# Pooled attention and experts on one core: the last 64 queries of each head as one block of upper and lower halves

## The chip, the cores and the metric

The kernel runs on one core of one Trainium2 chip. TensorE (PE) multiplies matrices, with its weight loads shown as a row of their own (PEld); VectorE (DVE), ScalarE (ACT) and GpSimd (POOL) do the element work; SyncE (SP) issues most of the DMA transfers. The metric is the device time of the whole program in microseconds (us), a median over runs.

## The reference

```python
def _attn_ref(q, k, v):                                  # 8 batches, 8 heads, 1152 rows, head size 64
    q_pool = q.reshape(B, H, S // 2, 2, D).mean(axis=3)  # 576 pooled queries
    scores = scale * np.matmul(q_pool, k.transpose(0, 1, 3, 2))
    scores = scores - np.max(scores, axis=-1, keepdims=True)
    attn = np.exp(scores)
    attn = attn / (np.sum(attn, axis=-1, keepdims=True) + 1e-09)
    return np.matmul(attn, v)

# x: the attention's output as 4608 tokens of 512
logits = x @ w_gate + modality_bias[modality_id]
e_idx = np.argmax(logits, axis=1)                        # one of 8 experts
gate_w = softmax(logits)[rows, e_idx]
out[mask] = gate_w[mask, None] * (np.maximum(x[mask] @ w1[e], 0) @ w2[e])
```

## The kernel before, in words

**Pairs and steps.** The 64 heads are worked in 32 pairs p of two heads j. A pair takes 18 steps, one for each head and each chunk c of 128 keys (9 chunks). After the pairs come the experts, which the change does not touch.

**Scores.** `scores(p, j, r)` (L865 on) makes the exponentials of a block r of three chunks: 3 × 576 = 1728 columns, for 128 keys on the partitions. A pair has six such blocks; where they are counted below, r0 to r2 are those of head 0 and r3 to r5 those of head 1. The columns are cut into four score tiles t of BANK = 432 columns, each in one of three PSUM buffers. A tile is two to four matmuls, L903 and L904 (b1 and b2 are the two parts that give the scores more than fp16 precision). ACT takes the exponential of each tile (L905) into `Pe`, as 32-bit integers scaled by 2^25. The upper 16 bits of such an integer are read as one fp16 matrix, Ph. The lower 16 bits are multiplied by 2^-24 into a second fp16 matrix `Pl`: 1152 columns by ACT after tile t = 2 (L886), and 576 by DVE one step after tile t = 3 (L888). There are four buffers (Pe, Pl), `PT[i % 4]`.

**Value products.** `pv(p, j, c)` (L948) follows three steps later (LAG). For a chunk it takes the 576 queries in five groups g of 128 columns as the stationary operand and makes three products for each: L962 (Ph with the values' upper part `vh`), L963 (Ph with `vl`), L964 (Pl with `vs`). The fifth group holds only 64 queries of its own; the other 64 columns of that block are padding (zeros, set once at the start) or a neighbour's. All nine chunks add up in one PSUM tile `xp`, whose column 64 is the sum of the exponentials. `evac` (L971) then divides: DVE L980, a reciprocal, and L985 into `x2`. `split_x` (ACT L922) rounds the result, and for odd p a DMA transpose of it (L946) is issued on SP.

**Work for later pairs.** While pair p−2 is computed, pair p is prepared: `split_q` (POOL L655, pools the queries), `split_qh` (POOL cast L664 to `qh`, followed by two DMAs that copy `qh` into the block matrix `QB`, issued on SP), `split_lo` (POOL L692, three times), and for pair p+1's values POOL L783, twice. `maxpass(p)` (L824) multiplies QB with the keys (PE L836), DVE L837 takes the maximum over the keys; the row of maxima goes back by a small DMA (L817). These are placed by a table of step numbers: the cast at T_QH = −26, which is step 10 of pair p−2, the first matmul of maxpass at T_MAX = −24, two steps later.

**What sets the order.** PE, ACT, DVE and POOL run their instructions in the order in which the program writes them: ORD, three strings, gives each step's order of score tiles (s), value products (v), maximum matmuls (M) and due work (F), and the T_ tables say at which step preparation is due. SP's queue order is not written by hand; it is chosen when the program is scheduled. On all of these engines the queue is worked in order, so an instruction that waits holds up those behind it.

Of the kernel before, what the change touches and what calls it, by code (L numbers as in the profile page):

```python
# [22 lines left out]
P = 128  # L23
# [16 lines left out]
NR = 4  # L40
W3 = 3 * SQ
HELD = 3
BANK = W3 // 4
T_LIST = -127
PL = 2
RS = (4, 4, 2, 2)
# [117 lines left out]
class Router:  # L164
# [420 lines left out]
def attention(tc, ctx, att, ident, npairs, xpool, on_two, on_split, on_scale, jobs, side, set_pm, started, ahead, hip):  # L585
# [163 lines left out]
    def scales(p, pt):  # L749
        s = st[p]  # L750
        half = sm.tile([P, 1], I32, name="half", bufs=1)
        nc.vector.tensor_single_scalar(half, pt[:, 0:1].bitcast(I32), 24, op=ALU.logical_shift_right)
        sc = sm.tile([P, 2], I32, name="sc")
        power_of = lambda o, h, sign, e: nc.vector.tensor_scalar(o, h, sign * 2.0 ** 23, e * 2.0 ** 23, op0=ALU.mult, op1=ALU.add)
# [111 lines left out]
    def scores(p, j, r):  # L866


        s = st[p]
        b1, b2 = s["B1"], B2[p % 2]  # L870
        i = (p * 2 + j) * 3 + r
        assert free[i % NR] == 0, "the value products of these exponentials come too late"
        free[i % NR] = 3
        Pe, Pl = PT[i % NR]
        word = lambda dt, w: Pe.bitcast(dt).rearrange("p (n w) -> p n w", w=2)[:, :, w]
        s["P", j, r] = (word(F16, 1), Pl, i % NR)
        lows = LOWS_LAST if p == npairs - 1 else LOWS_LIST[P_LIST[p]] if p in P_LIST else LOWS if p else LOWS0
        lows = lows[i % len(lows)]
        up = lambda a, b: slice(D + a, D + b) if j else slice(D + W3 - b, D + W3 - a)
        for m in range(3):  # L880
            later_end((LAG if p else LAG0) + m, lambda m=m: pvq.append(pv(p, j, 3 * r + m)))

        def lower(eng, cols):
            low, rest = Pl[:, cols], word(U16, 0)[:, cols]
            if eng == 'A':
                nc.scalar.activation(low, rest, AF.Copy, scale=LOW)  # L886
            else:
                fast[0] = (nc.vector if eng == 'D' else nc.gpsimd).tensor_single_scalar(low, rest, LOW, op=ALU.mult)  # L888

        for t in range(4):  # L890
            need(p, *(("place",) if p else ()), "row5" if j == 0 and (p == 0 or p in TWO_ROWS) else "row9")
            pt = ps_sc.tile([P, 512], F32, name="psc")[:, 0:BANK]
            x0 = t * BANK if j else W3 - (t + 1) * BANK
            x1 = x0 + BANK
            ms = [(x0 // SQ, x0, min(x1, (x0 // SQ + 1) * SQ))]
            if ms[0][2] < x1:
                ms.append((ms[0][0] + 1, ms[0][2], x1))
            for n, y0, y1 in ms if j else ms[::-1]:
                c = 3 * r + (n if j else 2 - n)
                ks = slice(j * S + c * P, j * S + (c + 1) * P)  # L900
                q0 = 2 * S + j * SQ - n * SQ
                qs, o = slice(q0 + y0, q0 + y1), pt[:, y0 - x0:y1 - x0]
                nc.tensor.matmul(o, b1[:, ks], b1[:, qs], start=True, stop=False, skip_group_check=True)  # L903
                nc.tensor.matmul(o, b2[:, ks], b2[:, qs], start=False, stop=True, skip_group_check=True)  # L904
            nc.scalar.activation(Pe[:, D + x0:D + x1], pt, AF.Exp, scale=1.0 / 16)  # L905
# [42 lines left out]
    def pv(p, j, c):  # L948
# [3 lines left out]
        vh, vs, vl = VH[p % 3], VS[p % 3], s["vl"]  # L952
        need(p, "vs", f"vl{int(c >= PARTS[1][1])}")
        Ph, Pl, i = s["P", j, c // 3]
        x = D + (c % 3 if j else 2 - c % 3) * SQ
        if c == 0:
            s["xp"] = ps_pv.tile([P, 512], F32, name="xp", tag="pv")[:, 0:5 * W].rearrange("p (g w) -> p g w", w=W)
        xp = s["xp"]
        for g in range(5):
            o = x + g * P + (D if j and g < 4 else -D - 4 * P if j else 0)  # L960
            qs, out = slice(o, o + P), xp[:, g, 0:D + 1]
            nc.tensor.matmul(out, Ph[:, qs], vh[:, c, j, 0:D + 1], start=c == 0 and g == 0, stop=False, skip_group_check=True)  # L962
            nc.tensor.matmul(out[:, 0:D], Ph[:, qs], vl[:, c, j], start=False, stop=False, skip_group_check=True)  # L963
            nc.tensor.matmul(out, Pl[:, qs], vs[:, c, j, 0:D + 1], start=False, stop=c == NKC - 1, skip_group_check=True)  # L964
# [37 lines left out]
    def later(n, fn):  # L1002
        todo.setdefault(max(now[0] + n, flushed[0] + 1), []).append(fn)
# [630 lines left out]
```

## Time and profile before

| | |
|---|---|
| median of three runs | 1129.57 us (1128.46 to 1130.51) |
| the profiled execution | 1128.8 us, of which the span takes 1127.1 us |
| granted TensorE clock, mean | 0.998 |
| PE busy | 1104.4 us |
| DVE busy | 973.7 us |
| ACT busy | 912.5 us |
| POOL busy | 416.2 us, 408 instructions |

The span runs from the first to the last instruction that the profiler saw; the rest of the profiled execution's own time, 1.7 us, lies around it. Busy time counts no waiting, no register work and no issuing of DMAs. A timeline row gives the start, the duration, the engine, the line and the operation with its tiles; a bracket behind it says how long the engine had been idle and what ended that. A row of the groups gives the count, then total busy time and the mean in nanoseconds, then idle time ahead of the group.

### The profile page before, as it was taken

How to read it: one execution, taken by the hardware profiler on the slowest of the kernel's cores; microseconds unless marked ns; L12 is line 12 of the kernel's file. 1: busy time of each engine (PE TensorE's matmuls, PEld its weight loads, DVE VectorE, ACT ScalarE, POOL GpSimd, SP SyncE). 2: the span in 40 equal slices, each digit the busy share in tenths (PEclk: the TensorE clock that was granted, in tenths of full speed). 3: DMA queues.
4: the chain of work that ended last, by engine and by line, in shares of the span. 5: the costliest groups of instructions: out<-in, count | busy, mean ns of one | idle time of the engine just before them, and what ended most of it. 6: DMA issues, size and time to landing. Idle time of an engine off the chain costs nothing. (4 is left out here: it accounts for less than half of the span.)

```text
span 1127.1 us, 36928 instructions
## 1 busy us (share of the span) xinstructions
PE 1104.4 (98%) x15117; PEld 813.9 (72%) x15117; DVE 973.7 (86%) x1968; ACT 912.5 (81%) x1462; POOL 416.2 (37%) x408
## 2 busy tenths in 40 slices
PE   8999999999999999999999999999999999999997
PEld 3777777777777777777777777767667667667665
DVE  7999999999999999999999999887986666756754
ACT  5999999999999999999999998865646666655654
POOL 7753344355434444443444343123113112122111
PEclk9999999999999999999999999999999999999999
DMA  7767757768769678678687573599989999999993
GB/s 233 189 177 173 192 160 185 193 154 185 177 161 207 158 179 179 172 173 198 165 188 167 148 166 76 172 292 282 282 259 260 279 317 271 275 278 263 287 276 107
DMA packets 175522, 232.67 MB, mean 206 GB/s; under 512 B 92303, under 2 KB 126751, under 8 KB 175344
## 3 DMA queue, kind: packets, MB, share of 16 engines
q1 hardware_dynamic: 169254, 210.45, 71.2%
q0 software_dynamic: 6080, 19.78, 6.9%
q8 instruction: 120, 1.97, 0.8%
q14 instruction: 58, 0.48, 0.1%
q10 hardware_dynamic: 10, 0.00, 0.0%
HBM read 146.11 MB, written 18.99 MB: 146 GB/s over the span
## 5 line engine op out<-in xcount | busy, mean ns | idle before, releaser
L905 ACT ACTIVATE Pe<-psc 128x432 int32<-128x432 f32 x768 | 376.6, 526 | 40.8 <-PE psc L904 32.4
L837 DVE TENSOR_REDUCE mp<-pm 128x1 f32<-128x512 f32 x566 | 371.6, 684 | 16.0 <-PE pm L836 9.2
L962 PE MATMUL xp<-VH,Pe 128*128 128x65 f16 x2880 | 372.9, 194 | 0.0
L964 PE MATMUL xp<-VS,Pl 128*128 128x65 f16 x2880 | 372.1, 193 | 0.4 <-DVE Pl L888 0.4
L963 PE MATMUL xp<-vl,Pe 128*128 128x64 f16 x2880 | 371.0, 192 | 0.0
L963 PEld LDWEIGHTS <-Pe 128*128 128x128 f16 x2880 | 267.6, 98 | 87.7
L903 PE MATMUL psc<-B 128*128 128x432 f16 (+2 forms) x1152 | 304.3, 286 | 1.6 <-ACT Pe L905 1.4
L904 PE MATMUL psc<-B 65*128 65x432 f16 (+2 forms) x1152 | 304.9, 287 | 0.1
L962 PEld LDWEIGHTS <-Pe 128*128 128x128 f16 x2880 | 271.9, 98 | 42.0 <-issue 4.3
L964 PEld LDWEIGHTS <-Pl 128*128 128x128 f16 x2880 | 266.6, 97 | 0.6 <-DVE Pl L888 0.5
L886 ACT ACTIVATE Pl<-Pe 128x1152 f16<-128x1152 uint16 (+1 forms) x190 | 219.3, 1154 | 6.0
L836 PE MATMUL pm<-hi,QB 128*128 128x512 f16 x566 | 214.0, 379 | 4.1 <-DVE mp L837 2.9
L1309 PE MATMUL ph<-xpart,w1h 128*128 128x256 f16 x544 | 148.4, 273 | 0.0
L1311 PE MATMUL ph<-xpart,w1l 128*128 128x256 f16 x544 | 148.4, 273 | 0.0
L1310 PE MATMUL ph<-xpart,w1h 128*128 128x256 f16 x544 | 148.3, 273 | 0.0
L783 POOL TENSOR_SCALAR VH<-rawv,sc 128x512 f16<-128x512 f32 (+1 forms) x60 | 103.6, 1736 | 76.3 <-PE pm L836 35.6
L904 PEld LDWEIGHTS <-B 65*128 65x128 f16 x1152 | 112.9, 98 | 25.1 <-issue 2.4
L903 PEld LDWEIGHTS <-B 128*128 128x128 f16 x1152 | 112.6, 98 | 7.9 <-issue 2.5
L1315 DVE SCALAR_TENSOR_TENSOR hl<-ph,hh 128x512 f16<-128x512 f32 x72 | 49.7, 690 | 75.8 <-ACT hh L1314 75.7
L1314 ACT ACTIVATE hh<-ph 128x512 f16<-128x512 f32 x72 | 43.0, 598 | 87.3 <-PE ph L1311 87.3
L1403 PE MATMUL po<-w2l,hh 128*128 128x512 f16 x288 | 109.2, 379 | 0.0
L1404 PE MATMUL po<-w2h,hl 128*128 128x512 f16 x288 | 109.2, 379 | 0.0
(276 smaller groups left out, 1894.4 us busy)
## 6 DMA issues: line engine op xcount, KB each, us to landing
w2r<-in_w_dram SPq DMA_DIRECT2D x76, 512.0 KB
w1r<-in_w_dram SPq DMA_DIRECT2D x72, 512.0 KB
rawv<-in_att_dram SPq DMA_DIRECT2D x32, 576.0 KB
B<-hi SPq DMA_DIRECT2D x128, 144.0 KB
rawq<-in_att_dram SPq DMA_DIRECT2D x31, 576.0 KB
rawk<-in_att_dram SPq DMA_DIRECT2D x31, 576.0 KB
B<-qh SPq DMA_DIRECT2D x128, 72.0 KB
B<-lo SPq DMA_DIRECT2D x64, 144.0 KB
```

The source lines that it names most:

```text
L836: nc.tensor.matmul(pm, QB[p % 2][:, u], s["hi"][:, t * 512:(t + 1) * 512], start=True, stop=True)
L837: nc.vector.tensor_reduce(mp[:, u, t:t + 1], pm, op=ALU.max, axis=AX.X)
L886: nc.scalar.activation(low, rest, AF.Copy, scale=LOW)
L903: nc.tensor.matmul(o, b1[:, ks], b1[:, qs], start=True, stop=False, skip_group_check=True)
L904: nc.tensor.matmul(o, b2[:, ks], b2[:, qs], start=False, stop=True, skip_group_check=True)
L905: nc.scalar.activation(Pe[:, D + x0:D + x1], pt, AF.Exp, scale=1.0 / 16)
L962: nc.tensor.matmul(out, Ph[:, qs], vh[:, c, j, 0:D + 1], start=c == 0 and g == 0, stop=False, skip_group_check=True)
L963: nc.tensor.matmul(out[:, 0:D], Ph[:, qs], vl[:, c, j], start=False, stop=False, skip_group_check=True)
L964: nc.tensor.matmul(out, Pl[:, qs], vs[:, c, j, 0:D + 1], start=False, stop=c == NKC - 1, skip_group_check=True)
L1309: nc.tensor.matmul(o, hi[:, c, fs], xh[:, :, c], start=c == 0, stop=False)
L1310: nc.tensor.matmul(o, hi[:, c, fs], xl[:, :, c], start=False, stop=False)
L1311: nc.tensor.matmul(o, lo[:, c, fs], xh[:, :, c], start=False, stop=c == 3)
```

## The change

**Tiles.** The columns of a block are laid out anew. Three of the four score tiles are now one chunk's first 512 queries (FULL), and tile t = 2 holds the last 64 queries of all three chunks, 192 columns. The number of score columns and of score matmuls stays the same (12 a block).

**The 64-query block.** The exponentials of tile t = 2 are written into the left halves of three blocks of 128 columns in `Pe`; a new POOL instruction (L910 of the changed kernel) writes their lower halves, times 2^-24, as fp16 into the right halves. So group g = 4 is one stationary block of 128 columns: 64 upper halves, 64 lower halves. It takes two products, with vh and with vl; the third one is left out, 9 times a head. The other lower halves are 1024 columns by ACT (now after t = 1) and 512 by DVE (after t = 3).

**Adding up.** The lower 64 rows of the fifth group in `xp` are the lower halves' share. A new step `rest_of` copies them on ACT times 2^-16, and one step later (EVL2) DVE adds them to the upper rows, at the head of `evac`; what follows evac moves with it. In `scales`, one DVE instruction fewer is made and another becomes a POOL copy. The 16 POOL instructions that set the padding at the start are gone.

```diff
-BANK = W3 // 4
+FULL = SQ - D
+W3F = 3 * FULL
+WP = W3F + 3 * P
...
-LOWS = (((0, 1152, 'A', 2), (1152, 1728, 'D', 3)), ((0, 1152, 'A', 2), (1152, 1728, 'D', 3)))
-LOWS_LAST = (((0, 864, 'D', 1), (864, 1728, 'D', 3)),)
+LOWS = (((0, 1024, 'A', 1), (1024, 1536, 'D', 3)),)
...
+EVL, EVL2 = 0, 1
...
-    PT = [(const.tile([P, W3 + 2 * D], I32, name=f"Pe{i}"), const.tile([P, W3 + 2 * D], F16, name=f"Pl{i}")) for i in range(NR)]
+    PT = [(const.tile([P, WP], I32, name=f"Pe{i}"), const.tile([P, W3F], F16, name=f"Pl{i}")) for i in range(NR)]
...
-        sc = sm.tile([P, 2], I32, name="sc")
+        sc, isc = sm.tile([P, 1], I32, name="sc"), on_scale(p)
         power_of = lambda o, h, sign, e: nc.vector.tensor_scalar(o, h, sign * 2.0 ** 23, e * 2.0 ** 23, op0=ALU.mult, op1=ALU.add)
-        power_of(sc[:, 0:1], half, -1, 205)
-        power_of(sc[:, 1:2], half, 1, 49)
-        s["sc"], s["isc"] = sc.bitcast(F32)[:, 0:1], sc.bitcast(F32)[:, 1:2]
-        on_scale(p, lambda o: power_of(o, half, 1, 49))
+        power_of(sc, half, -1, 205)
+        power_of(isc, half, 1, 49)
...
-        power_of(st[p - p % 2]["both"][r], half[r], 1, 49)
+        nc.gpsimd.tensor_copy(st[p - p % 2]["both"][r], isc[r])
...
-            pt = ps_sc.tile([P, 512], F32, name="psc")[:, 0:BANK]
-            x0 = t * BANK if j else W3 - (t + 1) * BANK
-            x1 = x0 + BANK
-            ms = [(x0 // SQ, x0, min(x1, (x0 // SQ + 1) * SQ))]
-            if ms[0][2] < x1:
-                ms.append((ms[0][0] + 1, ms[0][2], x1))
-            for n, y0, y1 in ms if j else ms[::-1]:
-                c = 3 * r + (n if j else 2 - n)
-                ks = slice(j * S + c * P, j * S + (c + 1) * P)
-                q0 = 2 * S + j * SQ - n * SQ
-                qs, o = slice(q0 + y0, q0 + y1), pt[:, y0 - x0:y1 - x0]
+            pt = ps_sc.tile([P, 512], F32, name="psc")
+            q0 = 2 * S + j * SQ
+            if t == 2:
+                q0 += 0 if j else FULL
+                ms = [(c, slice(q0, q0 + D), pt[:, c * D:(c + 1) * D]) for c in range(3)]
+            else:
+                q0 += D if j else 0
+                ms = [(min(t, 2), slice(q0, q0 + FULL), pt[:, 0:FULL])]
+            for c, qs, o in ms:
+                ks = slice(j * S + (3 * r + c) * P, j * S + (3 * r + c + 1) * P)
                 nc.tensor.matmul(o, b1[:, ks], b1[:, qs], start=True, stop=False, skip_group_check=True)
                 nc.tensor.matmul(o, b2[:, ks], b2[:, qs], start=False, stop=True, skip_group_check=True)
-            nc.scalar.activation(Pe[:, D + x0:D + x1], pt, AF.Exp, scale=1.0 / 16)
+            if t == 2:
+                o = Pe[:, W3F:].rearrange("p (c h n) -> p c h n", c=3, h=2)[:, :, 0]
+                nc.scalar.activation(o, pt[:, 0:3 * D].rearrange("p (c n) -> p c n", c=3), AF.Exp, scale=1.0 / 16)
+                nc.gpsimd.tensor_single_scalar(halves(F16, 1, 1), halves(U16, 0, 0), LOW, op=ALU.mult)
...
-        x = D + (c % 3 if j else 2 - c % 3) * SQ
...
-            o = x + g * P + (D if j and g < 4 else -D - 4 * P if j else 0)
-            qs, out = slice(o, o + P), xp[:, g, 0:D + 1]
-            nc.tensor.matmul(out, Ph[:, qs], vh[:, c, j, 0:D + 1], start=c == 0 and g == 0, stop=False, skip_group_check=True)
-            nc.tensor.matmul(out[:, 0:D], Ph[:, qs], vl[:, c, j], start=False, stop=False, skip_group_check=True)
-            nc.tensor.matmul(out, Pl[:, qs], vs[:, c, j, 0:D + 1], start=False, stop=c == NKC - 1, skip_group_check=True)
+            out, first, last = xp[:, g, 0:D + 1], c == 0 and g == 0, c == NKC - 1
+            o = c % 3 * FULL + g * P if g < 4 else W3F + c % 3 * P
+            qs = slice(o, o + P)
+            nc.tensor.matmul(out, Ph[:, qs], vh[:, c, j, 0:D + 1], start=first, stop=False, skip_group_check=True)
+            nc.tensor.matmul(out[:, 0:D], Ph[:, qs], vl[:, c, j], start=False, stop=last and g == 4, skip_group_check=True)
+            if g < 4:
+                nc.tensor.matmul(out, Pl[:, qs], vs[:, c, j, 0:D + 1], start=False, stop=last, skip_group_check=True)
             if g == 4:
                 free[i] -= 1
             if c == NKC - 1 and g == 4:
-                later(0, lambda: evac(p, j, xp))
+                later(EVL, lambda: rest_of(p, j, xp))
             yield
 
-    def evac(p, j, xp):
-
-        s = st[p]
+    def rest_of(p, j, xp):
+
+        low = sm.tile([D, D + 1], F32, name="low", bufs=2)
+        nc.scalar.activation(low, xp[D:P, 4, 0:D + 1], AF.Copy, scale=2.0 ** -16)
+        later(EVL2, lambda: evac(p, j, xp, low))
+
+    def evac(p, j, xp, low):
+
+        s = st[p]
+        nc.vector.tensor_tensor(xp[D:P, 4, 0:D + 1] if j else xp[0:D, 4, 0:D + 1], xp[0:D, 4, 0:D + 1], low, op=ALU.add)
...
-    for pe, pl in PT:
-        for x in (slice(0, D), slice(D + W3, 2 * D + W3)):
-            nc.gpsimd.memset(pe[:, x].bitcast(F32), 0.0)
-            nc.gpsimd.memset(pl[:, x], 0.0)
```

The new POOL instruction has no table entry: it is queued where its score tile is written. On POOL, from pair 10 (the cast is that of pair 12), what stands there before:

```order
L655 TENSOR_TENSOR rawq<-rawq 128x576
L783 TENSOR_SCALAR VH_127<-rawv,sc 128x8x64
L783 TENSOR_SCALAR VH_127<-rawv,sc 128x10x64
L664 CAST qh<-rawq 128x576
L692 TENSOR_TENSOR lo<-rawq,qh 128x576
L692 TENSOR_TENSOR lo<-rawk,hi 128x576
L310 TENSOR_SCALAR exp<-kmin 128x9
```

And now:

```order
L658 TENSOR_TENSOR rawq<-rawq 128x576
L785 TENSOR_SCALAR VH_127<-rawv,sc 128x8x64
L910 TENSOR_SCALAR Pe_117<-Pe_117 128x3x64
L785 TENSOR_SCALAR VH_127<-rawv,sc 128x10x64
L910 TENSOR_SCALAR Pe_119<-Pe_119 128x3x64
L910 TENSOR_SCALAR Pe_121<-Pe_121 128x3x64
L667 CAST qh<-rawq 128x576
L695 TENSOR_TENSOR lo<-rawq,qh 128x576
L695 TENSOR_TENSOR lo<-rawk,hi 128x576
```

The instruction of block r3 (Pe_121 here) stands directly ahead of the cast `qh`; those of r1 and r2 stand around the second value split, L783 of before and L785 now.

On SP in the same place (xs is the table of finished rows, xt the transposed output of pairs 8 and 9, `B_0` and `B_1` the operands of pairs 12 and 11), before:

```order
L645 DMA rawv<-in_att_dram 128x1152
L625 DMA QB_112<-qh 64x576 x2
L230 DMA xs<-x_5255 128x9x128
L625 DMA B_0_111<-qh 64x576
L640 DMA rawq<-in_att_dram 128x1152
L946 DMA_TRANSPOSE xt_6267<-x_5701 128x9x128
L817 DMA B_1_113<-mr 1x9x128
L946 DMA_TRANSPOSE xt_6268<-x_5702 128x9x128
```

And now:

```order
L648 DMA rawv<-in_att_dram 128x1152
L233 DMA xs<-x_5191 128x9x128
L954 DMA_TRANSPOSE xt_6202<-x_5645 128x9x128
L628 DMA QB_112<-qh 64x576 x2
L819 DMA B_1_113<-mr 1x9x128
L628 DMA B_0_111<-qh 64x576
L628 DMA B_0_111<-lo 64x1152
L954 DMA_TRANSPOSE xt_6203<-x_5646 128x9x128
```

The store to xs and the first transpose, which both stood behind the two QB copies, now stand ahead of them.

On ACT at block r3 of the same pair (x is the result of `split_x`), before:

```order
L905 ACTIVATE Pe_121<-psc 128x432 x2
L922 ACTIVATE x_5701<-x_5255,sc 128x9x64
L905 ACTIVATE Pe_121<-psc 128x432
L886 ACTIVATE Pl_122<-Pe_121 128x1152
L905 ACTIVATE Pe_121<-psc 128x432
```

And now:

```order
L913 ACTIVATE Pe_121<-psc 128x512 x2
L887 ACTIVATE Pl_122<-Pe_121 128x1024
L909 ACTIVATE Pe_121<-psc 128x3x64
L930 ACTIVATE x_5645<-x_5191,sc 128x9x64
L913 ACTIVATE Pe_121<-psc 128x512
```

The lower halves moved ahead of the exponential of tile t = 2, and `split_x` moved behind it. On PE the first matmul of maxpass keeps its place, directly behind tile t = 2 of block r4.

More of the change, by code (lines that the diff above doesn't have):

```diff
@@ L51 @@
 LD = 1
-LOWS = (((0, 1152, 'A', 2), (1152, 1728, 'D', 3)), ((0, 1152, 'A', 2), (1152, 1728, 'D', 3)))
-LOWS_LAST = (((0, 864, 'D', 1), (864, 1728, 'D', 3)),)
+LOWS = (((0, 1024, 'A', 1), (1024, 1536, 'D', 3)),)
+LOWS_LAST = (((0, 512, 'D', 0), (512, 1536, 'D', 3)),)
 P_LIST = {26: 0, 27: 0}
-LOWS_LIST = [tuple(((0, 1152, 'A', 2), (1152, 1728, e, 3)) for e in x) for x in ('DDA', 'DA', 'A')]
+LOWS_LIST = [tuple(((0, 1024, 'A', 1), (1024, 1536, e, 3)) for e in x) for x in ('DDA', 'DA', 'A')]
 D0 = 5
@@ L74 @@
 V1 = (9, 11, (14, 15), 18, (18, 19))
-LOWS0 = (((0, 1152, 'A', 2), (1152, 1728, 'D', 3)),)
+LOWS0 = LOWS
 LAG0 = 7
@@ L236, in gate_weights, with token_scale @@
         return w
-    def token_scale(self, p, isc):
+    def token_scale(self, p):
         g, h = divmod(p, H)
@@ L242, in token_scale @@
             self.scales[g] = self.keep.tile([P, H], I32, name="scales")
-        isc(self.scales[g][:, h:h + 1])
+        return self.scales[g][:, h:h + 1]
     def turned(self, x, o):
@@ L752, in scales @@
         nc.vector.tensor_single_scalar(half, pt[:, 0:1].bitcast(I32), 24, op=ALU.logical_shift_right)
-        sc = sm.tile([P, 2], I32, name="sc")
+        sc, isc = sm.tile([P, 1], I32, name="sc"), on_scale(p)
         power_of = lambda o, h, sign, e: nc.vector.tensor_scalar(o, h, sign * 2.0 ** 23, e * 2.0 ** 23, op0=ALU.mult, op1=ALU.add)
-        power_of(sc[:, 0:1], half, -1, 205)
-        power_of(sc[:, 1:2], half, 1, 49)
-        s["sc"], s["isc"] = sc.bitcast(F32)[:, 0:1], sc.bitcast(F32)[:, 1:2]
-        on_scale(p, lambda o: power_of(o, half, 1, 49))
+        power_of(sc, half, -1, 205)
+        power_of(isc, half, 1, 49)
+        s["sc"], s["isc"] = sc.bitcast(F32), isc.bitcast(F32)
         if p % 2 == 0:
@@ L878, in scores @@
         lows = lows[i % len(lows)]
-        up = lambda a, b: slice(D + a, D + b) if j else slice(D + W3 - b, D + W3 - a)
         for m in range(3):
@@ L887, in lower @@
             else:
-                fast[0] = (nc.vector if eng == 'D' else nc.gpsimd).tensor_single_scalar(low, rest, LOW, op=ALU.mult)
+                fast[0] = nc.vector.tensor_single_scalar(low, rest, LOW, op=ALU.mult)
+        halves = lambda dt, w, n: word(dt, w)[:, W3F:].rearrange("p (c h n) -> p c h n", c=3, h=2)[:, :, n]
         for t in range(4):
             need(p, *(("place",) if p else ()), "row5" if j == 0 and (p == 0 or p in TWO_ROWS) else "row9")
-            pt = ps_sc.tile([P, 512], F32, name="psc")[:, 0:BANK]
-            x0 = t * BANK if j else W3 - (t + 1) * BANK
-            x1 = x0 + BANK
-            ms = [(x0 // SQ, x0, min(x1, (x0 // SQ + 1) * SQ))]
-            if ms[0][2] < x1:
-                ms.append((ms[0][0] + 1, ms[0][2], x1))
-            for n, y0, y1 in ms if j else ms[::-1]:
-                c = 3 * r + (n if j else 2 - n)
-                ks = slice(j * S + c * P, j * S + (c + 1) * P)
-                q0 = 2 * S + j * SQ - n * SQ
-                qs, o = slice(q0 + y0, q0 + y1), pt[:, y0 - x0:y1 - x0]
+            pt = ps_sc.tile([P, 512], F32, name="psc")
[8 more added lines that the diff above has]
+                ks = slice(j * S + (3 * r + c) * P, j * S + (3 * r + c + 1) * P)
                 nc.tensor.matmul(o, b1[:, ks], b1[:, qs], start=True, stop=False, skip_group_check=True)
                 nc.tensor.matmul(o, b2[:, ks], b2[:, qs], start=False, stop=True, skip_group_check=True)
-            nc.scalar.activation(Pe[:, D + x0:D + x1], pt, AF.Exp, scale=1.0 / 16)
+            if t == 2:
+                o = Pe[:, W3F:].rearrange("p (c h n) -> p c h n", c=3, h=2)[:, :, 0]
+                nc.scalar.activation(o, pt[:, 0:3 * D].rearrange("p (c n) -> p c n", c=3), AF.Exp, scale=1.0 / 16)
+                nc.gpsimd.tensor_single_scalar(halves(F16, 1, 1), halves(U16, 0, 0), LOW, op=ALU.mult)
+            else:
+                c = ms[0][0]
+                nc.scalar.activation(Pe[:, c * FULL:(c + 1) * FULL], pt[:, 0:FULL], AF.Exp, scale=1.0 / 16)
             for y0, y1, eng, after in lows:
@@ L908, in scores @@
                     if eng == 'A':
-                        lower(eng, up(y0, y1))
+                        lower(eng, slice(y0, y1))
                     else:
-                        later(LD, lambda e=eng, y=up(y0, y1): lower(e, y))
+                        later(LD, lambda e=eng, y=slice(y0, y1): lower(e, y))
             if t < 3:
```

## The prediction

> **What bounds the kernel now.** I read the page's list of engines first, then the table of windows in the middle of the attention stage, then the groups, then the timeline around the change.
>
> ```profile
> PE 1104.4 (98%) x15117; PEld 813.9 (72%) x15117; DVE 973.7 (86%) x1968; ACT 912.5 (81%) x1462; POOL 416.2 (37%) x408
> 200.00:300.00 100.00, 99.95 (x1740) 77.38 (x1737) 96.46 (x221) 94.80 (x162) 46.48 (x42) 1.00 0.73 179
> 400.00:500.00 100.00, 99.95 (x1749) 77.63 (x1748) 96.38 (x222) 94.54 (x163) 47.11 (x43) 1.00 0.75 180
> ```
>
> PE is busy for 99.95 of each 100 us, DVE for 96.4, ACT for 94.7, POOL for 47, at a granted clock of 1.00. PE is the bound. A us that PE stands still is therefore lost, and nothing else has to be caught up for it. Busy PE time is not what a matmul costs, though, since matmuls overlap:
>
> ```profile
> L962 PE MATMUL xp<-VH,Pe 128*128 128x65 f16 x2880 | 372.9, 194 | 0.0
> L964 PE MATMUL xp<-VS,Pl 128*128 128x65 f16 x2880 | 372.1, 193 | 0.4 <-DVE Pl L888 0.4
> ...
> 401.32 0.19 PE L962 MATMUL xp<-VH,Pe 128*128 128x65 f16 x1
> ...
> 401.59 0.35 PE L903 MATMUL psc<-B 128*128 128x432 f16 x1
> ```
>
> A value product shows 193 ns, but between these two starts there are nine of them: 0.27 us / 9 = 30 ns each. That is the price of one.
>
> **The change part by part.**
>
> *Removed on PE.* One product of group g = 4 goes for each of 32 pairs × 2 heads × 9 chunks = 576. 576 × 30 ns = 17.3 us. The scores keep their count and their columns, so they stay at their price. In the sum: −17.3.
>
> *ACT, DVE and POOL in bulk.*
>
> ```profile
> L905 ACT ACTIVATE Pe<-psc 128x432 int32<-128x432 f32 x768 | 376.6, 526 | 40.8 <-PE psc L904 32.4
> L886 ACT ACTIVATE Pl<-Pe 128x1152 f16<-128x1152 uint16 x186 | 216.5, 1164 | 5.9
> L886 ACT ACTIVATE Pl<-Pe 128x576 f16<-128x576 uint16 x4 | 2.7, 684 | 0.1
> L985 DVE SCALAR_TENSOR_TENSOR x<-xp,sc,rr 64x64 f32<-64x64 f32 x32 | 9.3, 290 | 0.5
> L783 POOL TENSOR_SCALAR VH<-rawv,sc 128x640 f16<-128x640 f32 x30 | 57.2, 1906 | 0.0
> L783 POOL TENSOR_SCALAR VH<-rawv,sc 128x512 f16<-128x512 f32 x30 | 47.0, 1566 | 76.3 <-PE pm L836 35.6 <-PE xp L964 17.6 <-PE xp L962 14.8
> L754 DVE TENSOR_SCALAR both<-half 64x1 int32<-64x1 int32 x32 | 4.6, 142 | 0.2
> ```
>
> The two L886 rows give ACT (1164 − 684) / 576 = 0.83 ns an element, so its lower half of 1024 columns takes 1.06 us. That saves 6 × 0.107 = 0.64 us a pair, and two copies of 65 columns (0.526 − 367 × 0.00083 = 0.22 us each) take 0.44 back. DVE gains two adds a pair, 2 × 0.29 by the nearest row, and loses two tiny operations, 2 × 0.142: about 0.3 us on a pair of some 22 us, under its free 3.6%. POOL gains six L910. The two L783 rows give (1906 − 1566) / 128 = 2.66 ns an element and 206 ns fixed; 192 elements are then 0.72 us (estimate; bounds 0.3 and 0.95). That is 4.3 us a pair on an engine with 53% free. In the sum: nothing from any of the three as throughput. What hides L910 from the value products is LAG: they come three steps, over 3 us, behind the score tile. If that cover were too short, each pair would lose up to the 1.9 us of the POOL operation that stands ahead of it.
>
> *The cast behind L910, and who waits for it.* POOL works in order. The new instruction of block r3 stands directly ahead of the cast to `qh`, and so ahead of QB and of the first matmul of maxpass. Before, at pair 10:
>
> ```profile
> 254.58 0.66 POOL L664 CAST qh<-rawq 128x576 f16<-128x576 f32 x1
> 255.26 1.11 SPq L625 DMA_DIRECT2D QB<-qh  x2
> 256.46 0.54 SPq L230 DMA_DIRECT2D xs<-x  x1
> 257.28 0.29 PE L904 MATMUL psc<-B 65*128 65x288 f16 x1
> 257.99 0.23 PE L904 MATMUL psc<-B 65*128 65x144 f16 x1
> 258.03 0.77 ACT L922 ACTIVATE x<-x,sc 128x576 f16<-128x576 f32 x1
> 258.70 0.52 ACT L905 ACTIVATE Pe<-psc 128x432 int32<-128x432 f32 x1
> 259.31 1.34 SPq L946 DMA_TRANSPOSE xt<-x  x1
> 261.48 0.38 PE L836 MATMUL pm<-hi,QB 128*128 128x512 f16 x1
> ```
>
> The rows at 257.28 and 257.99 end tiles t = 1 and t = 2 of block r3; call the second end E = 258.22. The first maximum matmul on the new QB starts at 261.48, which is E + 3.26; 6.2 us lie between the end of the cast and that matmul. Afterwards the cast waits for this chain. Tile t = 1 ends at about E − 0.46 (0.65 before; tile t = 2 has fewer columns). Its exponential, 512 columns, takes 0.526 + 80 × 0.00083 = 0.59 us, to E + 0.13. ACT's lower half, which now comes first, ends at E + 1.2, and the exponential of 192 columns (0.33) at about E + 1.5. L910 follows to E + 2.28, the cast (0.66) to E + 2.93, and the issue on SP at E + 2.96. Then QB must land, L later. PE wants it at E + 3.3. PE stalls for L − 0.3.
>
> For L the trace has a neighbour, another plain transfer on SP, whose reader waits for it:
>
> ```profile
> 50.33 0.44 SPq L188 DMA_DIRECT2D idt<-in_ids_dram  x1
> 53.43 0.21 POOL L190 CAST mid<-idt 128x36 f32<-128x36 int32 x1 [0.83 <-DMA idt<-in_ids_dram]
> ```
>
> That is 3.1 us from issue to use; the lower bound is 0.44, the issue alone. I take 2.2, towards the upper end, since a row that includes the landing is nearer than one that leaves it out, and QB starts from a tile and not from a tensor in DRAM. [...]
>
> For odd p (14 pairs, p = 5 to 31), nothing else stands ahead on SP: stall 2.2 − 0.3 = 1.9 us, 14 × 1.9 = 26.6. In the sum: +26.6.
>
> *The transpose ahead of QB.* For even p (4 to 30, 14 pairs), SP's queue now holds the store to xs and the first transpose ahead of the two QB copies. The transpose waits for `split_x`, which now stands behind the exponential of t = 2: E + 1.5 + 0.77 = E + 2.25. Its issue holds SP for 1.3 us (row at 259.31), so QB is issued at E + 3.55 in place of E + 2.96. If the transfers run side by side, the stall is 3.55 + 2.2 − 3.3 = 2.45 us. If QB's packets queue behind those of the transpose, they land after it. For its size, 288 KB, the nearest row is a table store of twice that:
>
> ```profile
> xs<-x POOLq DMA_DIRECT2D x1, 576.0 KB, 7.3
> ```
>
> Half of that is 3.65 us, all of it 7.3; I take 4.5 from the transpose's issue, nearer the half because of the bytes. It lands at E + 6.75, QB 0.3 later, and the stall is 3.8 us. [...] 14 × 3.8 = 53.2. In the sum: +53.2.
>
> *The start.* In pair 1, POOL's one-time setup stands ahead of the L910 of block r2.
>
> ```profile
> 51.19 0.20 POOL L182 CAST wg<-wg 128x32 bf16<-128x32 f32 x1
> ...
> 58.14 0.20 PE L962 MATMUL xp<-VH,Pe 128*128 128x65 f16 x1
> ...
> 58.88 0.83 POOL L664 CAST qh<-rawq 128x576 f16<-128x576 f32 x1
> ```
>
> The setup runs from 51.19 to 58.88, directly behind other work. Four new L910 and two small copies ahead of it (4 × 0.72 + 2 × 0.2 = 3.3) push its end to 62.2, and that L910 ends at 62.9. PE wants the block at 58.14. In the sum: +4.8; without the push it would be 1.5.
>
> *Sum.* 1128.8 − 17.3 + 26.6 + 53.2 + 4.8 = 1196.1 us for the profiled execution, which was 0.8 below the median of the runs: 1197.
>
> **The rivals.**
>
> *The saving shows (faster).* If QB came in time, only the 17.3 and the start's 4.8 would be left: 1116 + 0.8 = 1117. It decides on the mean stall: 17.3 − 4.8 = 12.5 us over 28 pairs is 0.45 us a pair. The chain would have to be some 2.4 us shorter than I reckon, with a landing near its lower bound. For it speaks that I have no row of QB's landing; against it, the 3.1 us of the neighbour.
>
> *No queue behind the transpose.* Odd and even pairs then differ by the later issue alone, 14 × 1.9 + 14 × 2.45 = 60.9: 1177. For it: the transfers are spread over 16 engines. Against it: the DMA share of 0.73 in the windows leaves little free.
>
> *PE turns slow after a stall.* Rows from the program's start show that PE can run at half pace though the granted clock reads 1.00:
>
> ```profile
> 11.49 0.53 PE L859 MATMUL pm<-hi,QB 128*128 128x384 f16 x1
> ...
> 12.03 0.52 PE L859 MATMUL psc<-hi,QB 128*128 128x384 f16 x1
> 12.49 0.33 PE L859 MATMUL pm<-hi,QB 128*128 128x384 f16 x1
> 12.76 0.33 PE L859 MATMUL psc<-hi,QB 128*128 128x384 f16 x1
> ```
>
> With one filler matmul between each two, starts are 0.54 us apart at first and 0.27 from 12.49 on. If each stall of 3.8 us brought some 4 us at half pace, it would cost 2 us more in 14 pairs: 1197 + 28 = 1225. Against it: no attention stall in the trace is long enough to test it. [...]
>
> **How the numbers follow.** The main case has 0.57, with a range of its own of 1180 to 1222 (L at 1.7 takes 14 us off, L at 3.1 adds 25, L910 at 0.3 us takes 12 off). No queue behind the transpose: 0.2 (1177, and 1163 with L at 1.7). Slow PE: 0.08. The saving shows: 0.1. The 0.05 left are stalls that just cancel the saving. The range 1150 to 1226 leaves out the faster case, the stalls that only cancel the saving, and some of the slow PE's upper end. A measurement of this kernel can tell about 0.2%, 2.3 us, from no change. Faster 0.10, same 0.03, slower 0.87.
>
> **What would show it right or wrong.** Right: in the waits, PE L838 (the maximum matmul) waits for a DMA into QB some 28 times, about 2 us in odd pairs and nearly 4 in even ones; the cast L667 starts within 0.1 us of the end of a L910; PE is near 88% busy in the windows (79.8 us of stall over 28 pairs is 2.85 us on a pair of some 24). L910 at 0.7 us and the transpose's issue ahead of QB's are steps of their own. Wrong: PE still 99.9% busy between 200 and 300 us, or its waits on QB under 0.5 us; or waits on POOL's L910 in front of the value products in every pair.

## The result, and the profile after

The changed kernel takes 1242.81 us (median of five runs, 1241.56 to 1244.03), the kernel before, run beside it, 1130.51 (1128.46 to 1131.41). The ratio is 1.0999 with a 95% interval of 1.0986 to 1.1012: 112 us slower. The forecast was 1197, slower by 67, with a range up to 1226. So the sign was right and the size was not.

The page's list of engines of the changed kernel, and behind it its windows at the same two places as before:

```profile
PE 1129.2 (91%) x14541; PEld 764.4 (62%) x14541; DVE 1005.4 (81%) x1968; ACT 920.9 (74%) x1526; POOL 573.4 (46%) x616
```

```profile
200.00:300.00 100.00, 89.81 (x1417) 60.81 (x1415) 86.81 (x184) 82.01 (x146) 54.84 (x58) 0.96 0.60 149
400.00:500.00 100.00, 88.38 (x1380) 59.40 (x1379) 83.38 (x178) 80.48 (x146) 56.52 (x60) 0.95 0.57 145
```

PE makes 576 matmuls fewer and is busy 25 us longer. It stands still for 10 to 12 of each 100 us, where it stood for 0.05, and the granted clock (the column behind POOL) is 0.95 to 0.96 in place of 1.00. So there are two losses, waiting and a slower clock. PE's waits, with us in total, times, and the longest:

```profile
PE pm L838 <- DMA QB<-qh: 55.2, 28, 4.9
PE pm L838 <- DVE mp L839: 21.9, 46, 1.6
PE xp L970 <- POOL Pe L910: 4.6, 2, 4.2
```

The first row is the stall that was forecast, at the 28 pairs that were named. The third is the start, 4.6 us where 4.8 was reckoned. The second row is new: PE waits for VectorE to free the buffers of the maximum matmuls. Before, all waits of PE for DVE at these matmuls came to 4.7 us in the whole span.

The timeline of the changed kernel around an odd pair's first maximum matmul (p = 11) shows the chain that the prediction worked out:

```profile
271.56 0.19 PE L906 MATMUL psc<-B 65*128 65x64 f16 x1
271.96 1.06 ACT L887 ACTIVATE Pl<-Pe 128x1024 f16<-128x1024 uint16 x1
272.92 0.31 ACT L909 ACTIVATE Pe<-psc 128x192 int32<-128x192 f32 x1
273.31 0.75 POOL L910 TENSOR_SCALAR Pe<-Pe 128x192 f16<-128x192 uint16 x1 [3.80 <-ACT Pe L909]
273.98 0.66 POOL L667 CAST qh<-rawq 128x576 f16<-128x576 f32 x1
274.67 1.10 SPq L628 DMA_DIRECT2D QB<-qh  x2
276.63 0.39 PE L838 MATMUL pm<-hi,QB 128*128 128x512 f16 x1 [0.96 <-DMA QB<-qh]
```

E, the end of the score tile, is 271.75. The exponential ends at E + 1.48 (reckoned 1.5), the POOL instruction at E + 2.31 (2.28), the cast at E + 2.89 (2.93), and SP issues at E + 2.92 (2.96). QB is used 1.96 us after its issue (2.2 was taken). For the even pair behind it (p = 12):

```profile
298.48 1.33 SPq L954 DMA_TRANSPOSE xt<-x  x1
299.91 1.17 SPq L628 DMA_DIRECT2D QB<-qh  x2
...
302.46 0.39 PE L838 MATMUL pm<-hi,QB 128*128 128x512 f16 x1 [2.69 <-DMA QB<-qh]
```

The transpose is issued first, QB behind it, and QB is used 2.55 us after its issue: 0.6 us later than in the odd pair. Behind the transpose it does take longer, but it stays well under the 3.5 us from QB's issue that the forecast's queueing comes to.

The slower clock stands right behind such a stall. These are windows of the changed kernel behind the even pair's stall and behind the odd pair's; the clock is the number behind POOL's bracket:

```profile
302.40:304.00 1.60, 1.54 (x27) 1.13 (x28) 1.11 (x2) 0.23 (x2) 1.60 (x2) 0.88 0.21 48
304.00:307.20 3.20, 3.20 (x25) 1.56 (x23) 3.06 (x9) 1.19 (x2) 0.74 (x3) 0.53 0.35 75
307.20:309.20 2.00, 2.00 (x48) 1.52 (x45) 1.94 (x5) 1.91 (x4) 0.00 (x0) 1.00 1.06 197
...
276.60:278.60 2.00, 1.97 (x35) 1.38 (x36) 1.55 (x2) 1.72 (x5) 1.92 (x4) 1.00 0.64 106
```

After a wait of 2.69 us the clock is 0.53 for some three us and then 1.00 again. After a wait of 0.96 us it stays at 1.00. The length alone does not decide, as the eight us behind two other waits of this kind show, one of 2.54 us and one of 1.85:

```profile
353.30:361.30 8.00, 7.84 (x132) 5.35 (x133) 7.47 (x15) 5.95 (x11) 2.30 (x3) 1.00 0.71 186
378.30:386.30 8.00, 8.00 (x100) 5.07 (x101) 7.47 (x14) 4.49 (x9) 2.99 (x3) 0.79 0.63 181
```

Of the 28 waits on QB, 16 lasted 1.8 us or longer, and 12 of these were followed by such a slow stretch; none of the other 12, up to 1.47 us, was.

Last, the groups of DVE's two copies and of the new POOL instruction:

```profile
L889 DVE TENSOR_SCALAR Pl<-Pe 128x512 f16<-128x512 uint16 x188 | 106.4, 566 | 2.7 <-ACT Pe L913 1.5
L797 DVE TENSOR_SCALAR VS<-VH 128x1152 f16<-128x1152 f16 x31 | 18.0, 581 | 2.1 <-POOL VH L785 2.1
...
L910 POOL TENSOR_SCALAR Pe<-Pe 128x192 f16<-128x192 uint16 x192 | 157.1, 819 | 329.6 <-ACT Pe L909 328.5
```

The first has 512 columns where it had 576, and takes 566 ns where it took 511. The second is unchanged in the program and takes 581 ns where it took 487. Something outside these instructions draws them out. POOL has 157 us of new work.

### The profile page after: what moved, and what is told of

Same layout as the page of the kernel before. It is cut to its first block, busy times and chain, and to the rows that moved or that the text cites. A ratio compares the mean times of both kernels' runs of the same rounds, so it can differ in the third digit from the quotient of the medians.

```text
span 1240.1 us, 36204 instructions
## 1 busy us (share of the span) xinstructions
PE 1129.2 (91%) x14541; PEld 764.4 (62%) x14541; DVE 1005.4 (81%) x1968; ACT 920.9 (74%) x1526; POOL 573.4 (46%) x616
## 5 line engine op out<-in xcount | busy, mean ns | idle before, releaser
L839 DVE TENSOR_REDUCE mp<-pm 128x1 f32<-128x512 f32 x566 | 370.8, 684 | 80.2 <-PE pm L838 76.6
L913 ACT ACTIVATE Pe<-psc 128x512 int32<-128x512 f32 x576 | 332.4, 596 | 124.4 <-PE psc L906 110.6
L973 PE MATMUL xp<-VS,Pl 128*128 128x65 f16 x2304 | 316.0, 195 | 1.4 <-DVE Pl L889 1.4
L910 POOL TENSOR_SCALAR Pe<-Pe 128x192 f16<-128x192 uint16 x192 | 157.1, 819 | 329.6 <-ACT Pe L909 328.5
L906 PE MATMUL psc<-B 65*128 65x512 f16 (+1 forms) x1152 | 287.9, 293 | 0.8 <-DMA B<-mr 0.8
L905 PE MATMUL psc<-B 128*128 128x512 f16 (+1 forms) x1152 | 286.7, 292 | 1.6 <-ACT Pe L913 1.5
L973 PEld LDWEIGHTS <-Pl 128*128 128x128 f16 x2304 | 218.1, 98 | 1.8 <-DVE Pl L889 1.6
L887 ACT ACTIVATE Pl<-Pe 128x1024 f16<-128x1024 uint16 (+1 forms) x190 | 199.2, 1048 | 6.0
L1425 POOL DMA_INDIRECT out_dram<-o,siB x25 | 29.0, 1159 | 193.2 <-ACT o L1422 145.8
L889 DVE TENSOR_SCALAR Pl<-Pe 128x512 f16<-128x512 uint16 x194 | 110.9, 573 | 4.2 <-ACT Pe L913 3.0
L1305 DVE SCALAR_TENSOR_TENSOR w2l<-w2r,w2h 128x1024 f16<-128x1024 f32 x76 | 92.5, 1225 | 22.5 <-ACT w2h L1304 22.1
L785 POOL TENSOR_SCALAR VH<-rawv,sc 128x512 f16<-128x512 f32 (+1 forms) x60 | 103.7, 1728 | 12.4 <-DVE Pl L889 11.5
```

The lines of the kernel that those rows point to most:

```text
L839: nc.vector.tensor_reduce(mp[:, u, t:t + 1], pm, op=ALU.max, axis=AX.X)
L910: nc.gpsimd.tensor_single_scalar(halves(F16, 1, 1), halves(U16, 0, 0), LOW, op=ALU.mult)
L913: nc.scalar.activation(Pe[:, c * FULL:(c + 1) * FULL], pt[:, 0:FULL], AF.Exp, scale=1.0 / 16)
```

## The experiments

Each was timed beside the kernel before, whose median was 1129.9 to 1131.7 us. The theory after the result was: QB's lateness is POOL's order alone, the slow clock follows from it, and the rest is DVE, either through POOL or through the adding up.

**The cast one step earlier.**

```diff
-T_QH = -26
+T_QH = -27
```

> The changed kernel with one number altered: the cast to qh one step earlier (T_QH from -26 to -27), so that it stands in POOL's queue ahead of the new instruction of block r3, and SP issues QB ahead of the transpose. Theory: the wait of PE on QB (59.9 us between matmul starts in the changed kernel) comes from that order alone, and the slow stretches of PE (about 30 us) come from those waits; both go, 1242.8 - 60 - 30 = about 1153 us, clock back at 0.99 or more, and what is left above 1110 is the waits on DVE in front of other maximum matmuls (about 35 us). Rival A: those waits on DVE too are only an echo of the QB stall; then about 1115 us. Rival B: QB is late for another reason (its landing, SP); then no more than 20 us are gained, above 1220.

It took 1181.68 us, a ratio of 1.046 (1.0438 to 1.0481): 61 us of the 112 are gained. No wait on QB is left, and the clock is at 0.99. PE's waits:

```profile
PE pm L838 <- DVE mp L839: 24.1, 56, 1.5
PE pm L838 <- ACT hi L679: 9.2, 25, 0.7
PE xp L970 <- POOL Pe L910: 4.6, 2, 4.2
```

Rival B is out. Rival A is out too: with the QB stall gone, the waits on DVE are still there. The gain is 29 us under the theory's, and a part of that is named in the second row: the cast of the keys, which ACT now makes behind its lower halves, was hidden by the stall and comes late now.

**POOL's instruction alone, in the kernel before.**

```diff
+    spare = const.tile([P, 3, D], F16, name="spare")
...
             nc.scalar.activation(Pe[:, D + x0:D + x1], pt, AF.Exp, scale=1.0 / 16)
+            if t == 2:
+                nc.gpsimd.tensor_single_scalar(spare, word(U16, 0)[:, D + x0:D + x0 + 3 * D].rearrange("p (c n) -> p c n", c=3), LOW, op=ALU.mult)
```

> The kernel before with one thing added: after the exponential of tile t = 2 of each block POOL makes 128 x 3 x 64 low halves of it into a spare tile that nothing reads. So only the POOL instruction and its wait stand ahead of the cast; tiles, products, ACT's order and evac stay as they were. Theory: the stall on QB appears here too. ACT's exponential of t = 2 ends 1.0 us after the score tile here (not 1.5), so QB comes some 0.5 us sooner than in the changed kernel: 0.7 us a pair in odd pairs and up to 2 in even ones, 20 to 40 us in all, 1150 to 1170 us. Rival: the stall needs ACT's and SP's new order as well; then within 5 us of 1130.

It took 1206.07 us, 1.0672 (1.0654 to 1.069): 76 us more, twice what was expected. PE's wait on QB in it:

```profile
PE pm L837 <- DMA QB<-qh: 48.1, 28, 3.1
```

The stall is there, in the same 28 pairs. So the changed kernel's stall needs neither its tiles nor its products. But the 76 hold more than that wait.

**The same, with the cast earlier.** The edit is the one above plus T_QH = -27.

> The kernel of e2_pool_alone (1206.1 us: the kernel before plus POOL's 192 instructions into a spare tile) with the cast to qh one step earlier, so that no maximum matmul waits for QB. What is left over 1130 is what POOL's instructions cost through DVE alone, with before's tiles, products and evac. Theory: e2's 76 us are 53 us of QB stall, some 14 us of slow PE behind it and the rest DVE's drawn-out copies (Pl 646 ns against 511); so 1135 to 1165 us, more than 5 us above before. Rival: POOL does no harm to DVE that reaches PE; within 3 us of 1130, and the 35 us between e10 and e11 belong to the changed kernel's own order.

It took 1163.19 us, 1.0284 (1.0267 to 1.0301). Of the 76 us, 43 go with the order of the cast (1206.07 − 1163.19); 32 stay (1163.19 − 1131.65), with the kernel before in every other respect but the place of the cast. The earlier cast alone, without POOL's instructions, was not run, so it is not excluded that it has a part in the 32. Otherwise they are what the 192 instructions on POOL cost through DVE, which is now busy for 98.4 of 100 us (the third bracket):

```profile
200.00:300.00 100.00, 97.40 (x1657) 74.67 (x1654) 98.38 (x210) 91.78 (x155) 66.91 (x68) 1.00 0.67 163
```

The group of DVE's copies, 511 ns each in the kernel before, is 28.7 us longer in sum, and so accounts for most of the 32 by itself:

```profile
L889 DVE TENSOR_SCALAR Pl<-Pe 128x576 f16<-128x576 uint16 x182 | 121.7, 668 | 2.3 <-ACT Pe L906 1.2
```

The timeline of this kernel shows two of them, one beside an older POOL instruction and one beside a new one (L908):

```profile
247.45 1.80 POOL L693 TENSOR_TENSOR lo<-rawk,hi 128x576 f16<-128x576 f32 x1
248.02 1.54 DVE L889 TENSOR_SCALAR Pl<-Pe 128x576 f16<-128x576 uint16 x1
...
207.19 0.89 POOL L908 TENSOR_SCALAR spare<-Pe 128x192 f16<-128x192 uint16 x1 [1.34 <-ACT Pe L906]
207.43 0.45 DVE L889 TENSOR_SCALAR Pl<-Pe 128x576 f16<-128x576 uint16 x1
```

The copy of 576 columns that takes 0.45 us by itself takes 1.54 in the first case and lasts until 0.31 us after POOL's instruction has ended; in the second it takes its usual 0.45. Counted over the trace from 100 to 700 us: in the kernel before, 118 of 158 such copies meet no POOL instruction and take 450 ns on average, and 40 meet one and take 668. Here 104 of 152 meet one, and take 785. Of these, the 54 that meet only a new instruction take 484, and the 50 that meet an older one take 1110. So, by this count, it is hardly the new instructions themselves that hold up DVE: standing in POOL's queue, they move POOL's older work onto DVE's copies. No run tried other places for that older work.

**Two products instead of three, and nothing else.**

```diff
-            nc.tensor.matmul(out[:, 0:D], Ph[:, qs], vl[:, c, j], start=False, stop=False, skip_group_check=True)
-            nc.tensor.matmul(out, Pl[:, qs], vs[:, c, j, 0:D + 1], start=False, stop=c == NKC - 1, skip_group_check=True)
+            nc.tensor.matmul(out[:, 0:D], Ph[:, qs], vl[:, c, j], start=False, stop=c == NKC - 1 and g == 4, skip_group_check=True)
+            if g < 4:
+                nc.tensor.matmul(out, Pl[:, qs], vs[:, c, j, 0:D + 1], start=False, stop=c == NKC - 1, skip_group_check=True)
```

> The kernel before without the third value product of the fifth group (left out: the low halves of the last 64 queries of each head don't enter the output). Theory: 576 products at 30 ns go and nothing else changes: 17 to 20 us less, 1110 to 1113 us. Rival: DVE, busy 96 of 100 us, takes over as the bound; then less than half of it shows, 1120 us or more.

It took 1126.85 us, 0.9968 (0.9958 to 0.9978): 3.1 us less. By its number the rival holds: the saving alone, without any of the change's costs, is 3 us and not 17. Between 200 and 500 us PE stands still for 0.2 to 2.6 of each 100 us (0.05 to 0.07 before). Over the whole span its longest waits are for the row of maxima, which DVE makes and a DMA carries, and for DVE's maxima:

```profile
PE psc L904 <- DMA B<-mr: 4.1, 4, 2.1
PE pm L836 <- DVE mp L837: 3.9, 11, 0.6
PE pm L807 <- DVE m L803: 3.9, 7, 1.1
```

That DVE is the bound, as the rival has it, is not shown. PE's longest wait is 2.1 us, for the DMA; the clock is 0.98 between 200 and 300 us, where PE stands still for 2.6 us, and 1.00 in the next two windows; and DVE is busy for 94.0 to 97.2 of 100 us in these windows, less than the 98.4 above. The profiled execution took 1130.8 us, the longest of the nine, so it need not show what a typical one waits for. What takes up the other 14 us stays open.

**Fillers in the stall.**

```diff
+                if p > 3 and u == t == 0:
+                    for _ in range(5 if p % 2 else 9):
+                        nc.tensor.matmul(pm, zero[:, 0:P], zero, start=True, stop=True, skip_group_check=True)
                 nc.tensor.matmul(pm, QB[p % 2][:, u], s["hi"][:, t * 512:(t + 1) * 512], start=True, stop=True)
```

> The changed kernel with filler matmuls of 512 columns into the same PSUM tile directly ahead of each pair's first maximum matmul, five for odd p and nine for even p (0.216 us each: 1.1 and 1.9 us, within the measured stalls of 1.2 and 2.7 us). They keep PE busy for most of the time in which it would wait. Theory: the slow stretches follow the waits of 2 us and more; with the fillers they go, the clock reads 0.99 or more and the time falls by 20 to 30 us, to 1213 to 1223. Rival: the slow stretches have another cause; then the time stays within 3 us of 1242.8 or rises.

It took 1229.09 us against the changed kernel's 1242.81: 13.7 us less, though 196 more matmuls are made. PE's wait on QB falls to 13.2 us, and its list of cores reads

```profile
core 0: 1225.5 us, clock 0.994
```

where the changed kernel has 0.976. The sign and the clock are the theory's; the gain is 6 us under the 20 expected, and the waits on DVE's maxima, 24.5 us in place of 21.9, name only a part of that. PE's slow stretches do come from its own standing still.

**The new halves on ACT** (on the kernel with the early cast).

```diff
-                nc.gpsimd.tensor_single_scalar(halves(F16, 1, 1), halves(U16, 0, 0), LOW, op=ALU.mult)
+                nc.scalar.activation(halves(F16, 1, 1), halves(U16, 0, 0), AF.Copy, scale=LOW)
```

> The kernel of e1_cast_early (1181.7 us) with the new low halves of tile t = 2 made by ACT directly behind its exponential, not by POOL. Theory: DVE's fast copies (Pl: 623 ns on average in e1 against 506 before; VS: 637 against 450) are drawn out while POOL works, and that is a good part of the 60 us that PE waits in front of maximum matmuls; with the work on ACT, Pl is back near 490 ns and the time falls by 15 to 30 us, to 1152 to 1167. Rival: POOL has no part in it; Pl stays above 600 ns, ACT gets 1.5 us more a pair, and the time stays within 5 us of 1181.7 or rises.

It took 1194.1 us, 1.057 (1.0552 to 1.0588), 12 us worse than with POOL. DVE's copies are back at 474 ns, as the theory had it, but the time does not follow. DVE now stands still for something else, since ACT has the halves to make as well: the row for its add, waiting for ACT's copy of the lower rows, has grown from 20.6 us in the kernel with the early cast:

```profile
DVE xp L989 <- ACT low L983: 59.6, 57, 1.7
```

**Without the adding up.**

```diff
-                later(EVL, lambda: rest_of(p, j, xp))
+                later(0, lambda: evac(p, j, xp, None))
...
-        nc.vector.tensor_tensor(xp[D:P, 4, 0:D + 1] if j else xp[0:D, 4, 0:D + 1], xp[0:D, 4, 0:D + 1], low, op=ALU.add)
```

> The kernel of e1_cast_early without the adding up (left out: ACT's copy of the lower rows and DVE's add; the output of the last 64 queries of each head is not what it should be), with evac back in its old step. Theory: DVE stands behind the copy that waits in ACT's queue, and evac now comes where the last maxima of a pair are due; without it the waits in front of maximum matmuls 14 to 17 of a pair (36 us in e1) fall by at least half, 1181.7 - 18 to 36 = 1146 to 1164 us. Rival: evac's place costs nothing and those waits come from the spacing of the matmuls around the small tile or from POOL; then less than 8 us are gained.

It took 1174.98 us, 1.0398 (1.0381 to 1.0416): 6.7 us gained, under the rival's 8. By itself it is not the cause of the waits, with DVE's copies beside POOL's work still at 725 ns on average.

**ACT's lower halves late again, and both edits.**

```diff
-LOWS = (((0, 1024, 'A', 1), (1024, 1536, 'D', 3)),)
+LOWS = (((0, 1024, 'A', 2), (1024, 1536, 'D', 3)),)
...
-LOWS_LIST = [tuple(((0, 1024, 'A', 1), (1024, 1536, e, 3)) for e in x) for x in ('DDA', 'DA', 'A')]
+LOWS_LIST = [tuple(((0, 1024, 'A', 2), (1024, 1536, e, 3)) for e in x) for x in ('DDA', 'DA', 'A')]
```

> The kernel of e1_cast_early with ACT's lower halves again behind the exponential of tile t = 2 (as before the change) instead of ahead of it. Theory: ahead of it they hold up the second cast of hi by 1.06 us, for which the second maximum matmul of each pair waits (13.8 us in e1, 28 times); that wait goes, 1181.7 - 13 = about 1168 us. Rival: the wait moves to what comes next on ACT; less than 5 us are gained.

1180.11 us, 1.045 (1.0432 to 1.0467). PE's wait for the keys' cast is gone, and the time stays: the rival holds, and a wait on DVE took its place (L809 on DVE, 11.9 us).

> Both edits together on e1_cast_early: low halves of tile t = 2 on ACT, ACT's other lower halves behind tile t = 2. Theory: the two gains add up, 1140 to 1155 us. Rival: ACT, with 1.5 us more a pair, becomes the engine that PE waits for, and the sum is smaller than the two gains.

1179.48 us, 1.0443 (1.0426 to 1.0461). There was no gain from either edit alone to add up; against the kernel with only the halves on ACT it is 15 us less, against the one with only the late lower halves nothing. Its timeline shows what holds DVE:

```profile
276.88 1.03 ACT L887 ACTIVATE Pl<-Pe 128x1024 f16<-128x1024 uint16 x1
278.14 0.22 ACT L983 ACTIVATE low<-xp 64x65 f32<-64x65 f32 x1
278.40 0.22 DVE L989 TENSOR_TENSOR xp<-xp,low 64x65 f32<-64x65 f32 x1 [1.36 <-ACT low L983]
279.75 1.28 DVE L839 TENSOR_REDUCE mp<-pm 128x1 f32<-128x512 f32 x2
280.48 0.38 PE L838 MATMUL pm<-hi,QB 128*128 128x512 f16 x1 [0.73 <-DVE mp L839]
```

ACT's copy stands in its queue behind other work; DVE's add waits for it 1.36 us at the head of DVE's queue; the maxima behind it come late; PE waits for their buffer.

**DVE makes the copy itself.**

```diff
-        nc.scalar.activation(low, xp[D:P, 4, 0:D + 1], AF.Copy, scale=2.0 ** -16)
-        later(EVL2, lambda: evac(p, j, xp, low))
+        nc.vector.tensor_single_scalar(low, xp[D:P, 4, 0:D + 1], 2.0 ** -16, op=ALU.mult)
+        evac(p, j, xp, low)
```

> The kernel of e9_act_and_late (1179.5 us) with the lower rows of the fifth group copied by DVE itself and evac at once behind it, in its old step; ACT has no part in the adding up. Theory: DVE stood still for 37 us behind ACT's copy (up to 1.5 us each time), and PE waits for the maxima that are late for it; the copy costs DVE 0.2 us a head, 13 us in all of its own time, but no waiting: 1179.5 - 37 + up to 13 = 1142 to 1156 us, and the waits in front of maximum matmuls 4 and 14 of a pair (37 us in e9) fall below 10. Rival: DVE is full anyway and the waits only move to other maxima; then less than 10 us are gained.

With the halves on ACT it took 1141.25 us, 1.0092 (1.0074 to 1.011): 38 us less by one edit that gives DVE more work. The edit also puts `evac` back in its old step, one earlier; its place and the wait for ACT's copy are not told apart. The wait of PE for DVE's maxima falls from 36.6 us to

```profile
PE pm L838 <- DVE mp L839: 7.5, 21, 0.9
```

> The same edit on the kernel of e7_lower_late (1180.1 us), in which POOL makes the low halves of tile t = 2. Theory: DVE's waiting behind ACT's copy goes here too (some 20 us), but DVE's fast copies stay drawn out by POOL (Pl about 620 ns, VS about 615), some 1 us a pair: 1160 to 1170 us, 12 to 25 above e10_dve_copies. Rival: POOL's share of DVE's time costs nothing once DVE waits for nobody; then within 5 us of e10.

With the halves on POOL the same edit gave 1176.63 us, 1.0413 (1.0396 to 1.0431), 3.5 us under the kernel that it stands on and 35 above the one with ACT. PE's wait in this kernel, the group of DVE's copies, and one of its windows:

```profile
PE pm L838 <- DVE mp L839: 33.9, 52, 1.8
```

```profile
L889 DVE TENSOR_SCALAR Pl<-Pe 128x512 f16<-128x512 uint16 x188 | 111.2, 592 | 0.8
```

```profile
400.00:500.00 100.00, 94.08 (x1547) 64.75 (x1546) 97.80 (x217) 85.48 (x153) 64.28 (x69) 1.00 0.65 167
```

DVE is busy for 97.8 of 100 us here, in the whole span it waits for PE's maximum matmuls for only 11.8 us and for no copy of ACT's lower rows, and PE waits for DVE. So either of two things is enough to make DVE late: POOL's work beside its copies, or the wait for ACT's copy. Taking one away alone gave 4 us or less (1180.1 to 1179.5, and 1180.1 to 1176.6); both together gave 39. The two are not independent: with the halves on ACT, DVE's wait for ACT's copy rises from 17.0 us to 37.3.

**Two maxima further apart.**

```diff
-ORD = ('NvJMvsvMsvXF', 'JvvsMvvXFvv', 'vFvvsJvXv')
+ORD = ('NvJMvsvMsvXF', 'JvvsvMvXFvv', 'vFvvsJvXv')
```

> The kernel of e10_dve_copies with one letter of the order moved: in the second step of three, the maximum matmul comes one chunk of value products later, so that not only the small score tile lies between it and the one ahead. Theory: the 0.24 us that PE waits at maximum matmul 17 of nearly every pair (and part of those at 16) come from two maxima too close together; 5 to 15 us less than e10. Rival: DVE's total work decides and not the spacing; within 3 us of e10.

It took 1140.7 us, 1.0099 (1.0082 to 1.0116), the same as without it. The spacing around the small tile costs nothing that shows. No version tried beats the kernel before, other than the one with work left out.

## Why the prediction was right in its sign and wrong in its size

*Removed on PE, −17.3.* This step failed. The saving was booked as time because PE was busy for 99.95 of 100 us, and "nothing else has to be caught up for it". Alone, the removal gives 3.1 us. DVE, at 96, is the nearest candidate for what takes the rest, but that is not shown.

*ACT, DVE and POOL in bulk, "nothing from any of the three as throughput".* This is the step that failed most. It counted POOL's 4.3 us a pair against POOL's free time and DVE's 0.3 us against DVE's free 3.6%. It did not ask what a changed order on POOL does to DVE's copies, nor that a wait at the head of DVE's queue uses up the same 3.6%: 1.36 us of some 22 is 6%. POOL's new instructions are worth 32 us in the kernel before, with the earlier cast, and 39 go from the changed kernel with the earlier cast when both are taken away. In the changed kernel as it stands, DVE waits for ACT's copy for only 7.2 us, beside 76.6 for PE's late maximum matmuls. The price of L910 itself, 0.72 us, was near: 0.75 in the chain above, 0.82 in the mean.

*The cast behind L910, +26.6, and the transpose, +53.2.* The mechanism was right, step for step, and the sizes were too large: between the starts of the matmuls, beyond what lies there without a wait, the odd pairs lose 19.6 us and the even ones 40.1. For the odd pairs the landing was right on average: over the fourteen, QB is used 2.22 us after its issue where 2.2 was reckoned, the author's choice between 0.44 and 3.1 (2.00 in the middle, 1.96 in the pair above, and three took 2.75 to 3.81). What was off is when PE reaches the matmul: it begins to wait at E + 3.9 (276.63 − 0.96), where the sum had E + 3.3. For the even pairs it was the landing: 2.64 on average (2.34 in the middle, 2.55 in the pair above) where the sum had 3.5 (4.5 from the transpose's issue, less 1.3, plus 0.3). That QB lands only after the transpose was the author's estimate and no run shows it; the medians are 2.34 us behind a transpose and 2.00 without one. Of the two cases for the transpose, the one with no queueing (2.45 us of stall) was nearer to the 2.9 us that the even pairs lose on average (40.1 over 14).

*The start, +4.8.* Right: 4.6.

*PE turns slow after a stall.* It was given 0.08 and it happened, behind waits shorter than the 3.8 us that it was priced for: 12 of 16 waits of 1.8 us or more were enough. The 4 us at half pace in its price were the author's estimate; behind the even pair's wait above, the clock is 0.53 for 3.2 us. The fillers gave back 13.7 us; by the mean clocks, an estimate, (1 − 0.976) × 1240 = 30 us of full speed were lost in the changed kernel and (1 − 0.994) × 1225 = 7 with the fillers.

*The other side.* The saving could not show: its point of decision was a mean stall of 0.45 us a pair, and even the odd pairs lost 1.4 (19.6 over 14). The 88% of busy PE that was forecast for the windows came about (89.8 and 88.4), but as less stall on QB with waits on DVE beside it.

The sum as measured: the order of the cast 61 us (QB and the slow clock, less the waits that come in their place), POOL and the waiting of DVE 39 to 40 (among them the start's 4.6, whose wait is for POOL's instruction), and 11 are left (1141 against 1130). Those 11 are not settled. The kernel that has them makes its halves on ACT and its copy on DVE, so DVE and ACT are each busy for about 97 of 100 us there, and no run separated the new tiles from that.

## What to carry to other kernels

Before booking a saving on the busiest engine, take it away alone and see what is left: 3.1 us of 17.3 here. Beside an engine that is busy for 96% there is little room: on DVE, one wait of 1.36 us at the head of the queue was 6% of a pair, where 3.6% were free. A new instruction on an engine with time to spare (POOL, busy for 47 of 100 us) had three prices here beside its own 0.82 us: what stood behind it in that queue (the order of the cast, 61 us), what older work of that queue it moved onto the work of another engine (DVE's copies took 1110 ns beside that work and 484 beside the new instruction alone), and which engine had to wait for which from then on (PE for POOL at the start, 4.6 us). Two causes that each kept DVE late hid each other, 4 us or less for either one and 39 for both, so remove them together before calling either one harmless.

## What the runs showed of the hardware that was not expected

A PE wait of 2.69 us was followed by some three us at about half clock (0.53 in the window above), and one of 0.96 us was not; waits of 1.8 us and more did it 12 times of 16. A DVE copy of 0.45 us took up to 1.54 beside one kind of POOL instruction (576 columns of 32-bit input) and 0.44 to 0.63 beside another (192 columns of 16-bit input). Two transfers of 64 rows each, issued on SP right behind a transpose of 288 KB, were used after 2.34 us (the median of fourteen), only 0.3 later than those with no transpose ahead of them (2.00).
